# Attention and feed-forward in two layers: four heads of one key tile in one score phase

## The chip, the cores and the metric

The kernel runs on one core of one Trainium2 chip. The metric is the device time of one execution in microseconds (us). TensorE is PE in the profile (its weight loads PEld), VectorE is DVE, ScalarE is ACT, GpSimd is POOL and SyncE, which issues the transfers, is SP.

## The reference

Two layers, each an attention block and a feed-forward block with residuals, over 2048 tokens of width 512 in bf16. Attention has 32 heads of 16 channels and no mask.

```python
def _A_ref(x, wqkv, wo):
    qkv = (x @ wqkv).reshape(B, S, 3, H, Dh)          # H = 32, Dh = 16
    ...
    scores = einsum("bhqd,bhkd->bhqk", q, k) * Dh ** -0.5
    p = softmax(scores, axis=-1)
    o = einsum("bhqk,bhkd->bhqd", p, v)
    return merge_heads(o) @ wo
def _B_ref(x, w1, w2):
    return silu(x @ w1) @ w2
x = A_x
x = x + _A_ref(_layernorm(x), A_wqkv, A_wo)
x = x + _B_ref(_layernorm(x), B_w1, B_w2)
... # the same once more with the same weights
```

## The kernel before

**Blocks.** Attention is cut into blocks: one head, one key tile of 128 keys, one chunk of 512 queries. The scores of a block are one matmul (`score`, L754) with 32 rows of contraction (two heads share 32 rows, and a mask in `QT` picks one of them), which uses one of four row lanes of PE. A block is named by layer L, query chunk qc, pass pi, group of eight heads g, parity par, key tile kt and lane j. A run is all blocks of one (L, qc, pi, g, par): the four heads of lanes 0 to 3 over the key tiles of the pass. There are 4096 blocks: 2 layers x 4 chunks x 8 (g, par) x 16 key tiles x 4 lanes. A pass is all 16 key tiles, except where the keys are not made yet: the first chunk of layer 0 has passes of 4, 4 and 8 tiles, that of layer 1 of 12 and 4.

**Two ways to the exponential.** An A block's scores go to a PSUM tile `s_ps` of two banks (two blocks, two buffers), and ScalarE makes the exponentials with one ACTIVATE of 1024 columns (L1020) into `p_sb`. A D block's scores go to `d_ps` (one bank, two buffers); VectorE makes one fixed-point operation of it (L889, called the fix below), `d_y`, whose bits are read as a half float, and GpSimd adds two offset copies of a pair of these (`d_z0`, `d_z1`, L909). The sum of the three terms, each with its own scaled V (`VA`, and `VB` from `scale_v`), stands for the exponential. So an A block has one PV matmul, and a D block three. PV matmuls (L836) use four column lanes and add up into one bank `o_ps`; a column of ones in V gives the softmax sum. When a run ends, DVE copies `o_ps` (L992, `oT`, or `oA` and `oB` for passes), and PE turns it back (`att`, L467).

**Steps.** `plan` writes 1552 steps by hand: in each, two A blocks of a run, and in 992 of them also a D block, four steps or so ahead of where its run stands, whose lane is free in that step. Every second step or so is followed by PV for the two steps before (`emit_pv`), with terms of D blocks added where they are ready. `emit_pv` also puts in matmuls with zero weights (fills) where PE has had less than `FULL_CLOCK` groups of work since the last PV.

**Background.** All else is made of generators in one queue, `Background`: layer norm (`ln_stats`, `ln_apply`, `ln_transpose`), the projections for K, Q and V (`mm4`: four matmuls in two parts, then a DVE copy), the output projection, the feed-forward block with its 98 tanh on ScalarE (L526; 14 more stand in the tail). Each generator says before each part how much PE or DVE time it takes, and whether it holds the one PSUM bank `m` that all of them share. `Model` keeps an estimate of when each engine will be free, and the loop over steps puts a part into the order only where the model says that it fits before the next exp. What a step needs and what hasn't been made is forced by `Background.ensure`, whatever it costs.

**Order.** The engines work strictly in the order in which the loop emits (a manual schedule). In a step: the sum's copy, DVE parts, scores of the A blocks, score and fix of the D block, PV, PE parts, exp. SP takes its transfers in order as well: Q is brought into place with eight small transfers for each group of heads, `wo` is loaded again for each chunk into the buffer that `hT` and the pass sums (`oB`) use too. The last chunk's output projection and feed-forward form a `tail` after the steps.

Of the kernel before, what the change touches and what calls it, by code (L numbers as in the profile page):

```python
# [26 lines left out]
class Background:  # L27
# [3 lines left out]
    def __init__(self):  # L31
        self.queue = deque()
        self.urgent = deque()
        self.active = None
        self.done = {None}

# [36 lines left out]
    def ensure(self, label):  # L73
        while label not in self.done:
            self.advance(self.prime(self.active or self.queue[0]))

class Model:

    EXP = 0.947
    TANH = 0.66
    SWITCH = 0.09

    def __init__(self, slack, margin):
        self.slack, self.margin = slack, margin
        self.ends = [0.0, 0.0]
        self.pe = self.dve = self.ready = self.free = 0.0
        self.mode = None  # L90
# [6 lines left out]
    def begin(self, d):  # L97
        self.start = max(self.pe, self.ends[0] + 0.06)
        self.d = d

    def dve_fits(self, held, pe, dve):

        if dve == 0:
            if held:
                self.ends[1] = max(self.ends[1], self.ready) + self.TANH
                self.ready = self.ends[1] + 0.05
            return True
        end = max(self.dve, self.start, self.ready if held else 0.0) + dve
        if max(end, self.start + 0.4) + 0.69 * self.d > self.start + self.slack:
            return False  # L110
        self.dve = end
        if held:
            self.free = end
        return True

    def scores(self, d):
        self.pe = self.start
        self.to("S")
        self.pe += 0.25
        self.scored = self.pe + 0.06  # L120
        if d:
            self.dve = max(self.dve, self.pe + 0.1) + 0.69
# [4 lines left out]
    def pv(self, groups):  # L127
        self.to("V")
        self.pe += 0.224 * groups
        self.summed = self.pe + 0.1  # L130

    def pe_fits(self, pe):

        end = max(self.pe, self.free + 0.06) + pe + self.SWITCH * (self.mode != "B")
        act = max(self.ends[1], self.scored) + self.EXP
        if max(end + self.SWITCH, self.ends[1] + 0.06) + 0.31 + self.margin > act:
            return False
        self.pe, self.mode = end, "B"
        self.ready = end + 0.07
        return True  # L140

    def exp(self):
        self.ends = [self.ends[1], max(self.ends[1], self.scored) + self.EXP]

@with_exitstack
def kernel(
# [26 lines left out]
    VW = 17 * H + 16  # L173
    SHIFT = 2.0
# [10 lines left out]
    D_KTS = ((0, 5, 10, 15), (3, 4, 9, 14), (2, 7, 8, 12, 13), (1, 6, 11, 12, 14))  # L185

    FULL_CLOCK = 3


    DVE_SLACK = 2.2  # L190
    PE_MARGIN = 0.1


    STEPS = {16: (24, 23), 12: (20, 20), 8: (12, 12), 4: (7, 7)}
# [11 lines left out]
    ppool = ctx.enter_context(tc.tile_pool(name="ppool", bufs=5))  # L206
# [231 lines left out]
    def d_blocks(c):  # L438

        return [(kt, j) for kt in range(4 * c, 4 * c + 4) for j in range(4) if kt in D_KTS[j]]  # L440

    def scale_v(L, c):

        n = len(d_blocks(c))
        VB[L, c] = vbpool.tile(
            [P, n, 2, 8 * 17 + 16], FP16, name="VB", tag=f"VB{n}", bufs=6 if n == 4 else 1
        )
        nc.gpsimd.memset(VB[L, c][:, :, :, 8 * 17 :], 0.0)
        for i, (kt, j) in enumerate(d_blocks(c)):
            va = VA[L, c][:, kt % 4, 0 : 17 * H].rearrange("p (g j e) -> p g j e", j=4, e=34)  # L450
            for k, (_, w) in enumerate(TERMS):
                nc.gpsimd.tensor_scalar(
                    out=VB[L, c][:, i, k, 0 : 8 * 17].rearrange("p (g e) -> p g e", e=34),
                    in0=va[:, :, j, :],
                    scalar1=w,
                    scalar2=0.0,
                    op0=ALU.mult,
                    op1=ALU.add,
                )
# [217 lines left out]
    def lanes_of(n):  # L677
        return [(n + 3 - j) // 4 for j in range(4)]

    def plan():  # L680

        steps = []
        spans = []
        pv = {}
        for r in runs:
            key, kts = r[0:5], list(r[5])
            t0 = len(steps)  # L690
            t1 = t0 + STEPS[len(kts)][not (0, 1) <= key[0:2] <= (1, 0)]
            left = [len(kts) - m for m in lanes_of(2 * (t1 - t0))]
            d_rows = [[kt for kt in D_KTS[j] if kt in kts][: left[j]] for j in range(4)]
            assert [len(rows) for rows in d_rows] == left
            a_rows = [[kt for kt in kts if kt not in d_rows[j]] for j in range(4)]
            for i in range(0, 2 * (t1 - t0), 2):
                steps.append(([(*key, a_rows[m % 4][m // 4], m % 4) for m in (i, i + 1)], []))
            spans.append((t0, t1, key, d_rows))
            ends = [*range(t0 + 2, t1 - 1, 2), t1]
            for a, b in zip([t0, *ends], ends):  # L700
                pv[b + 1] = list(range(a, b))
        for t0, t1, key, d_rows in spans:
            ts = [t for t in range(max(0, t0 - D_LEAD), t1 - D_LEAD)]
            free = {t: [j for j in range(4) if j not in [b[6] for b in steps[t][0]]] for t in ts}
            n = sum(map(len, d_rows))
            lane = None
            for some in sorted(
                itertools.combinations(ts, n),
                key=lambda some: sum((b - a) ** 2 for a, b in zip((ts[0] - 1, *some), (*some, ts[-1] + 1))),
            ):  # L710
                lane = match(sorted(some, key=lambda t: len(free[t])), free, [len(rows) for rows in d_rows])
                if lane is not None:
                    break
            for t in sorted(lane):
                steps[t][1].append((*key, d_rows[lane[t]].pop(0), lane[t]))
        return steps, pv

    def match(ts, free, left):

        if not ts:  # L720
            return {}
        for j in sorted(free[ts[0]], key=lambda j: -left[j]):
            if left[j]:
                rest = match(ts[1:], free, [m - (k == j) for k, m in enumerate(left)])
                if rest is not None:
                    return {ts[0]: j, **rest}
        return None
# [3 lines left out]
    for ts in pv_steps.values():  # L731
        key = steps[ts[0]][0][0][0:5]
# [29 lines left out]
    def pv_block(blk, k, rhs):  # L762
# [6 lines left out]
        else:  # L769
            h = 2 * g + par  # L770
            i = d_blocks(kt // 4).index((kt, j))
            lhsT = VB[L, kt // 4][:, i, k - 1, 17 * h : 17 * h + 32]
        return (blk[0:5], j, lhsT, rhs)

    def pv_step(t):
        p_sb = p_tiles.pop(t)
        mms = []
        for i, blk in enumerate(steps[t][0]):
            mms.append(pv_block(blk, 0, p_sb[:, i, :]))
        return mms  # L780

    def emit_pv(t, mms, busy):
# [63 lines left out]
        fill = max(0, min(fill, 2))  # L846
# [12 lines left out]
        if ends:  # L859
# [16 lines left out]
            if final[key]:  # L876
                need = ("aT", *((L, qc - 1) if qc else (L - 1, NC - 1))) if (L, qc) != (0, 0) else None
                bg.urgent.append((t + 2, end_group(L, qc, g, par), need))
        return real + fill

    def emit_d(t, blk):

        s_ps = psum["s"].tile([P, 512], FP32, name="d_ps", tag="sd", bufs=2)
# [20 lines left out]
    def other_terms(t, pr):  # L904

        n = len(pr["ds"])
        for k, (off, _) in enumerate(TERMS):
# [9 lines left out]
            for i, d in enumerate(pr["ds"]):  # L917
                d["rhs"].append((t + 4 + k, k + 1, z[:, i, :].bitcast(FP16)))
# [14 lines left out]
    with tc.manual_schedule(  # L933
# [37 lines left out]
        begun = set()  # L971
        busy = 0.0
        m = Model(DVE_SLACK, PE_MARGIN)
        for t, (a_blks, d_blks) in enumerate(steps):
            for L, qc, pi, g, par, kt, j in d_blks + a_blks:
                bg.ensure(("q", L, qc, g))
                if qc == 0:
                    bg.ensure(("k", L, kt // 4, g))
            for L, qc, pi, g, par, kt, j in a_blks:
                if kt % 4 or j > 1 or (L, qc, pi, g, par, kt) in begun:  # L980
                    continue
                begun.add((L, qc, pi, g, par, kt))
                if par == 0 and (kt, g, pi) == (0, 0, 0):
                    attn[L, qc] = apool.tile([P, 4, D], BF16, name="attn", tag="attn")
                    if (L, qc) != (0, 0):
                        next_q(*((L, qc - 1) if qc else (L - 1, NC - 1)), NG - 1)
                first = PASSES.get((L, qc), [range(NKT)])[-1][0]
                if par == 0 and kt == first and g > 0 and final[L, qc, pi, g, par]:
                    next_q(L, qc, g - 1)
            m.begin(len(d_blks))  # L990
            while after:
                after.pop()()  # L992
                m.sums()

            while True:
                item = bg.head(t)
                if item is None or item[2][1] or not m.dve_fits(*item[2]):
                    break
                last = item[2][2] == 0
                bg.advance(item)  # L1000
                if last:
                    break
            s_ps = psum["s"].tile([P, 2, 512], FP32, name="s_ps", tag="s", bufs=2)
# [61 lines left out]
```

The softmax here doesn't subtract the row's maximum and nothing guards it: scores larger than these inputs give would overflow.

## Time and profile before

| | |
|---|---|
| median of three runs | 1609.77 us (1609.59 to 1619.6) |
| span of the profiled execution | 1605.9 us |
| ACT busy | 1514.0 us, 94% |
| PE busy | 1436.8 us, 89% |
| POOL busy | 1098.4 us, 68% |
| DVE busy | 1036.7 us, 65% |
| mean granted clock of PE | 0.986 |
| ACT idle just before exps | 47.4 us |

The profile gives no time of its own for the profiled execution beside its span, which runs from the first to the last instruction; the runs' times are measured around the whole execution, 3.9 us more at the median. An engine's busy time counts overlapping instructions once; neighbours overlap by some 0.1 us on ACT and more on PE, so an instruction's duration is longer than its distance to the next. In a group's row the numbers after the bar are busy time, the mean duration of one in ns, and the engine's idle time just before them with what ended it. A timeline row gives the start, the time covered, the engine, the line, what is written from what, and how many equal neighbours were merged.

### The profile page before, as it was taken

Reading aid. Unit: us, or ns where it says so; the run is one execution under the profiler, and the core shown is the slowest. Engines: PE = TensorE matmul, PEld = TensorE weight load, DVE = VectorE, ACT = ScalarE, POOL = GpSimd, SP = SyncE. Lnnn points to the kernel's source line nnn. Section 1 sums busy time; section 2 is a strip of 40 time slices with the busy share of each in tenths; the row PEclk is TensorE's granted clock in tenths of the full one; section 3 lists DMA queues with packets and bytes.
Section 4 is the critical chain, followed back from the end, with each engine's and each line's share of the span. In section 5 each row is a group of like instructions: output and inputs, shape, how many; then the busy total and the mean of one; then the engine's idle time right before and its main releaser. Section 6 shows DMA issues by size and latency. Waiting matters only on the chain.

```text
span 1605.9 us, 33881 instructions
## 1 busy us (share of the span) xinstructions
PE 1436.8 (89%) x12965; PEld 439.9 (27%) x12965; DVE 1036.7 (65%) x1729; ACT 1514.0 (94%) x1671; POOL 1098.4 (68%) x1160
## 2 busy tenths in 40 slices
PE   7889888899988999889998997888988899988988
PEld 3222222222222222222222222322222222222223
DVE  5566657567776668656664453776678667777644
ACT  6999989999999999999999998999999999999982
POOL 3447767677876778668743452788888788888860
PEclk9999999999999999999999998999999999999999
DMA  4000010101100001100011000100011101100011
GB/s 125 14 14 2 8 44 11 28 8 30 28 21 18 11 27 28 28 14 25 11 37 27 11 17 8 30 21 18 12 31 30 28 8 31 31 21 18 11 28 49
DMA packets 83506, 38.62 MB, mean 24 GB/s; under 512 B 63632, under 2 KB 82832, under 8 KB 83344
## 3 DMA queue, kind: packets, MB, share of 16 engines
q1 hardware_dynamic: 83344, 36.46, 8.6%
q8 instruction: 101, 1.65, 0.4%
q14 instruction: 61, 0.50, 0.1%
HBM read 28.57 MB, written 4.19 MB: 20 GB/s over the span
## 4 chain that ended last, share of the span: by engine, by line
ACT 43%; PE 33%; issue 11%; DVE 10%; DMA 1%; SPq 1%; POOL 1%; ACTq 0%; DVEq 0%
ACT p_sb L1020 40%; PE s_ps L754 10%; PE o_ps L836 10%; PE f_ps L586 4%; DVE d_y L889 3%; ACT t_sb L526 2%; PE h_ps L373 2%; DVE hT L529 1%; PE v_ps L373 1%; DVE xn L310 1%; DVE st L301 1%; PE y_ps L373 1%; PE k_ps L373 1%; PE q_ps L373 1%; SPq L414 1%
## 5 line engine op out<-in xcount | busy, mean ns | idle before, releaser
L1020 ACT ACTIVATE p_sb<-s_ps 128x1024 bf16<-128x1024 f32 x1552 | 1464.9, 1047 | 47.4 <-PE s_ps L754 26.7
L889 DVE TENSOR_SCALAR d_y<-d_ps 128x512 uint16<-128x512 f32 x992 | 674.4, 687 | 376.7 <-PE d_ps L754 338.1
L754 PE MATMUL s_ps<-QT,KT 32*128 32x512 bf16 x3104 | 602.8, 387 | 68.8 <-ACT p_sb L1020 62.6
L754 PE MATMUL d_ps<-QT,KT 32*128 32x512 bf16 x992 | 382.6, 386 | 0.5 <-DVE QT L405 0.5
L754 PEld LDWEIGHTS <-KT 32*128 32x128 bf16 x4096 | 160.7, 91 | 653.5 <-issue 640.8
L836 PE MATMUL o_ps<-p_sb,VA 128*32 128x512 bf16 x3104 | 316.0, 395 | 6.9 <-DVE oT L992 2.6
L836 PE MATMUL o_ps<-d_y,VA 128*32 128x512 f16 x992 | 176.0, 382 | 0.0
L836 PEld LDWEIGHTS <-VA 128*32 128x32 bf16 x4096 | 101.1, 94 | 190.5 <-issue 180.8
L586 PE MATMUL f_ps<-w_sb,hT 128*128 128x512 bf16 x392 | 112.8, 383 | 4.8 <-DVE hT L529 4.8
L836 PE MATMUL o_ps<-w_qkv,zero 128*32 128x512 bf16 x570 | 113.1, 383 | 0.0
L529 DVE SCALAR_TENSOR_TENSOR hT<-t_sb,h_ps 128x512 bf16<-128x512 f32 x98 | 67.3, 687 | 37.6 <-ACT t_sb L526 35.4
L836 PEld LDWEIGHTS <-VB 128*32 128x32 f16 x1984 | 75.4, 98 | 29.6 <-issue 6.0
L526 ACT ACTIVATE t_sb<-h_ps 128x512 f32<-128x512 f32 x98 | 60.3, 615 | 0.0
L992 DVE CAST oT<-o_ps 128x512 bf16<-128x512 f32 x63 | 43.1, 684 | 11.8 <-PE o_ps L836 11.7
L301 DVE BATCH_NORM_STATS2 st<-x 128x6 f32<-128x512 bf16 x64 | 43.4, 678 | 1.9 <-DMA x<-in_A_x_dram 1.9
L373 PE MATMUL y_ps<-wo,aT 128*128 128x512 bf16 x128 | 37.4, 394 | 4.3 <-DMA wo<-in_A_wo_dram 3.9
L373 PE MATMUL v_ps<-w_qkv,xnT 128*128 128x512 bf16 x128 | 37.4, 390 | 3.0 <-DVE VA L431 3.0
L373 PE MATMUL q_ps<-xnT,w_qkv 128*128 128x512 bf16 x128 | 38.1, 398 | 1.4 <-DVE KT L389 1.4
L586 PEld LDWEIGHTS <-hT 128*128 128x128 bf16 x392 | 25.6, 97 | 50.0 <-issue 40.2
L373 PE MATMUL k_ps<-xnT,w_qkv 128*128 128x512 bf16 x128 | 36.1, 382 | 2.9 <-DVE xnT L336 0.9
L467 PE MATMUL att<-ident,oT 128*128 128x128 bf16 x256 | 29.8, 223 | 8.6 <-DVE hT L529 8.3
L332 PE MATMUL t_ps<-ident,xn 128*128 128x128 bf16 x256 | 23.4, 226 | 15.3 <-DVE xn L310 14.9
(2269 smaller groups left out, 2149.0 us busy)
## 6 DMA issues: line engine op xcount, KB each, us to landing
wo<-in_A_wo_dram SPq DMA_DIRECT2D x8, 512.0 KB, 3.9
x<-in_A_x_dram SPq DMA_DIRECT2D x7, 512.0 KB, 4.4
QT<-q SPq DMA_DIRECT2D x224, 16.0 KB, 1.8
out_dram<-x SPq DMA_DIRECT2D x16, 128.0 KB, 1.7
w_sb<-in_B_w_dram SPq DMA_DIRECT2D x1, 1792.0 KB, 13.7
w_qkv<-in_A_wqkv_dram SPq DMA_DIRECT2D x3, 512.0 KB, 7.2
x<-in_A_x_dram SPq DMA_DIRECT2D x2, 256.0 KB, 3.1
x_0_113<-x SPq DMA_DIRECT2D x4, 128.0 KB, 1.8
```

What stands on the lines that cost most here:

```text
L301: nc.vector.bn_stats(st[:], x_sb[c][:, i, :])
L332: nc.tensor.transpose(t_ps[:, ct, u, :], xns[u][:, ct * P : (ct + 1) * P], ident[:, :])
L373: nc.tensor.matmul(ps, lhsT=lhs(ct), rhs=rhs(ct), start=(ct == 0), stop=(ct == CT - 1))
L467: nc.tensor.matmul(att[:, tq, :, :].rearrange("p j s -> p (j s)"), lhsT=o[:, tq * P : (tq + 1) * P], rhs=ident[:, :], start=(i == 0), stop ...
L526: nc.scalar.activation(t_sb, h_ps, ACT.Tanh, scale=0.5)
L529: nc.vector.scalar_tensor_tensor(out=hT[:, ft, :], in0=t_sb, scalar=1.0, in1=h_ps, op0=ALU.add, op1=ALU.mult)
L586: nc.tensor.matmul(y_ps, lhsT=hT[:, ft, tq * P : (tq + 1) * P], rhs=w2_sb[:, ft, :], start=(ft == 0), stop=(ft == FT - 1),)
L754: nc.tensor.matmul(out, lhsT=KT[L, kt // 4][r, g, (kt % 4) * P : (kt % 4 + 1) * P], rhs=QT[g][r, par, :], start=True, stop=True,)
L836: nc.tensor.matmul(o_tiles[key][32 * j : 32 * j + 32, :], lhsT=lhsT, rhs=rhs, start=(n[j] == 0), stop=stop,)
L889: nc.vector.tensor_scalar(out=pr["y"][:, len(pr["ds"]), :], in0=s_ps[:], scalar1=float(1024 * SCALE * math.log2(math.e)), scalar2=float(10 ...
L992: after.pop()()
L1020: nc.scalar.activation(p_tiles[t][:].rearrange("p a b -> p (a b)"), s_ps[:].rearrange("p a b -> p (a b)"), ACT.Exp, bias=-SHIFT * math.log ...
```

## The change

- A step becomes a batch: the four blocks (lanes 0 to 3) of one key tile of a run. There are 1024 batches. The block of lane kt % 4 is always a D block; the three others are A blocks. So 25% of the blocks are D blocks, where it was 24.2%; the first four D blocks are A blocks too, with two 1024-column exps ahead of the loop (`p_pre`).
- PSUM: `s_ps` keeps two buffers of two banks and holds two A blocks; the third A block has a bank of its own, `s1`, with one buffer. `d_ps` has one buffer instead of two. `o` and `m` keep one bank each.
- In each score phase: two matmuls to `s_ps`, one to `s1`, and one to `d_ps`, for the D block four batches ahead. ScalarE then does an exp of 512 columns on `s1` and one of 1024 on `s_ps`, into a `p_sb` tile of three banks' width, four buffers instead of five.
- PV comes every second batch, for the two batches before last. `FULL_CLOCK` goes from 3 to 5 groups and the bound on fills from 2 to 3.
- `Model` has other constants and keeps account of the new banks. Background parts, those of DVE too, are put in after the exps of a batch, and several of one batch may follow each other; parts forced by `ensure` are now charged to the model.
- `VB` is laid out without gaps between terms.

The order of the new kernel's instructions has these counts: 1024 exps of 512 and 1026 of 1024 columns, 1020 D blocks, 1252 fill matmuls (570 before), and the same background work and transfers.

```diff
+    EXP1 = 0.49
+    EXP2 = 0.918
+    TANH = 0.63
...
+    def scores(self, n, d):
         self.to("S")
+        self.pe = max(self.pe, self.s1, self.s2[n % 2])
+        self.scored = self.pe + self.GROUP + self.LAND
         if d:
+            self.pe = max(self.pe, self.sd)
+            self.dve = max(self.dve, self.pe + self.GROUP + self.LAND) + self.FIX
+            self.sd = self.dve + self.SEM
+        self.pe += self.GROUP
...
+    def fits(self, cost):
+        held, pe, dve = cost
+        if pe:
+            end = max(self.pe, self.free) + pe + self.SWITCH * (self.mode != "B")
+            return end + self.SWITCH + self.GROUP + self.LAND + self.margin <= self.act
+        if dve:
+            return max(self.dve, self.ready if held else 0.0) + dve <= self.act + self.slack
         return True
...
-    FULL_CLOCK = 3
-    DVE_SLACK = 2.2
-    PE_MARGIN = 0.1
-    STEPS = {16: (24, 23), 12: (20, 20), 8: (12, 12), 4: (7, 7)}
+    FULL_CLOCK = 5
+    DVE_SLACK = 0.0
+    PE_MARGIN = 0.05
...
-    ppool = ctx.enter_context(tc.tile_pool(name="ppool", bufs=5))
+    ppool = ctx.enter_context(tc.tile_pool(name="ppool", bufs=4))
...
     def plan():
+        blocks = [[(*r[0:5], kt, j) for j in range(4)] for r in runs for kt in r[5]]
+        d_of = [b[b[0][5] % 4] for b in blocks]
+        steps = [(d_of[0:D_LEAD], [])]
         pv = {}
+        for i, b in enumerate(blocks):
+            a = [b[(b[0][5] + k) % 4] for k in (1, 2, 3)]
+            steps.append((a, d_of[i + D_LEAD : i + D_LEAD + 1]))
+            pv.setdefault(i // 2 * 2 + 4, []).extend(
+                [(i + 1, k) for k in range(3)] + [(0, i)] * (i < D_LEAD)
+            )
         return steps, pv
...
-        fill = max(0, min(fill, 2))
+        fill = max(0, min(fill, 3))
...
-        s_ps = psum["s"].tile([P, 512], FP32, name="d_ps", tag="sd", bufs=2)
+        s_ps = psum["s"].tile([P, 512], FP32, name="d_ps", tag="sd", bufs=1)
...
+            s2 = score_pair()
+            s1 = psum["s"].tile([P, 512], FP32, name="s1_ps", tag="s1", bufs=1)
+            for i in range(2):
+                score(a_blks[1 + i], s2[:, i, :])
+            score(a_blks[0], s1[:])
+            for blk in d_blks:
+                emit_d(t, blk)
+            m.scores(t, len(d_blks))
+            while after:
+                after.pop()()
+                m.sums()
+            if t in pv_steps:
+                m.pv(emit_pv(t, pv_step(t), busy))
+                busy = 0.0
+            p_tiles[t] = ppool.tile([P, 3, 512], BF16, name="p_sb", tag="p")
+            exp(p_tiles[t][:, 0, :], s1[:])
+            exp(flat(p_tiles[t][:, 1:3, :]), flat(s2[:]))
+            m.exps(t)
+            while True:
+                item = bg.head(t)
+                if item is None or not m.fits(item[2]):
+                    break
+                m.charge(item[2])
+                busy += item[2][1] / 0.216
+                bg.advance(item)
```

## The prediction

> **What bounds the kernel now.** I read the page first (chain, then groups), then the timelines of ACT and of PE, then windows of 3.4 us for the clock.
>
> ```profile
> ACT 43%; PE 33%; issue 11%; DVE 10%; DMA 1%; SPq 1%; POOL 1%; ACTq 0%; DVEq 0%
> ...
> L1020 ACT ACTIVATE p_sb<-s_ps 128x1024 bf16<-128x1024 f32 x1552 | 1464.9, 1047 | 47.4 <-PE s_ps L754 26.7
> L889 DVE TENSOR_SCALAR d_y<-d_ps 128x512 uint16<-128x512 f32 x992 | 674.4, 687 | 376.7 <-PE d_ps L754 338.1
> ```
>
> ACT and PE share the chain. ACT is busy 94% of the span, but busy is not packed:
>
> ```profile
> 1060.78 0.60 ACT L526 ACTIVATE t_sb<-h_ps 128x512 f32<-128x512 f32 x1
> 1061.25 4.71 ACT L1020 ACTIVATE p_sb<-s_ps 128x1024 bf16<-128x1024 f32 x5
> 1065.77 0.68 ACT L526 ACTIVATE t_sb<-h_ps 128x512 f32<-128x512 f32 x1
> ```
>
> Start to start, five exps take 4.52, that is 0.904 each, though one shows 1.02 (neighbours overlap). A 512-wide tanh takes 0.477 to the next start. Both fit 0.050 fixed plus 0.427 per 512 columns. The exps start at 14.08 and the last at 1559.15, so the stream takes 1546.0. Packed it would be 1552 x 0.904 + 98 x 0.477 = 1449.7, so **96.2 us are lost between exps**: 20.1 up to the 209th exp (222.3, the end of the first query chunk), 76.1 after. Who loses them shows on PE:
>
> ```profile
> 498.12 0.39 PE L754 MATMUL s_ps<-QT,KT 32*128 32x512 bf16 x2
> ...
> 498.44 0.40 PE L836 MATMUL o_ps<-p_sb,VA 128*32 128x512 bf16 x4
> ...
> 498.66 0.39 PE L836 MATMUL o_ps<-d_y,VA 128*32 128x512 f16 x4
> ...
> 498.99 0.39 PE L754 MATMUL s_ps<-QT,KT 32*128 32x512 bf16 x2
> ...
> 499.31 0.60 PE L373 MATMUL h_ps<-fT,w_7555 128*128 128x512 bf16 x2
> ...
> 499.84 0.39 PE L754 MATMUL s_ps<-QT,KT 32*128 32x512 bf16 x2
> ```
>
> A score phase costs 0.32 whether it holds two or three blocks (0.216 of array time and 0.10 for the change of phase); PV costs 0.216 a group of four and 0.12; two background matmuls cost 0.54. Set against the order of the instructions, PE work after the first chunk is 92% of packed ACT time, and 146 of 1343 steps hold over 0.25 us more PE work than their exp lasts. So PE overload makes most of the 76.
>
> **The change, part by part.** All 4096 blocks stay.
>
> *ACT.* 1552 exps become 1024 of two banks, 1024 of one bank and 2 ahead of the loop. No 512-wide exp is in this trace; its bounds are half of a 1024-wide exp (0.452) and the tanh of that shape plus the 0.017 by which a quarter of the exps start late (0.921 for 0.904), 0.494. I take the tanh's own 0.477, the nearest row, since the fixed 0.050 is the same in both rows. Packed: 1024 x (0.904 + 0.477) + 1.8 + 46.7 = 1462.7, so **+12.9** (-13 and +30 at the bounds). The Trainium skill, "ScalarE: Activation LUTs", section "What ACT_TABLE_LOAD costs", speaks against this: an ACTIVATE with a bias pointer takes about 280 ns + 0.833 ns a column, and neighbours overlap by 93 ns. That leaves 187 ns fixed an instruction, and the 498 more would cost +81 net of the columns saved. By it the total below would be 1664; the rows show 50 ns fixed, so I keep theirs.
>
> *PE.* 1552 score phases become 1025 (-527 x 0.32 = -169); PV keeps its blocks but fills grow from 570 to 1252 matmuls (+170 groups x 0.216 = +37). The fourth lane in a score phase isn't in the trace; two lanes and three cost the same to 4 ns, so I take nothing. The upper bound, a whole 0.216 a batch, adds 194 after the first chunk and brings PE to 93% of ACT, where it was; the later losses would then stay near 76, the bound that I keep for them below. After the first chunk PE work falls from 92% to 78% of packed ACT time, and the batches over by more than 0.25 from 146 to 31. Why 0.25: s1 has one bank, so scores of batch t+1 wait for the one-bank exp of batch t (0.60 long), 0.05 more for the semaphore, and 0.49 from there to the next exp (28.17 to 28.66 below), together 1.14 of the 1.381 of a batch. Behind the waiting s1 score stand the fourth score, PV and background on PE, and the next exp. New waits of the score's weight load on PE's own matmuls are for those of two batches before, long done, and p_sb's four buffers are free a batch before they are needed; nothing for either.
>
> *d_ps with one bank.* Scores to fix 0.45, fix 0.69, semaphore 0.05: 1.19 of 1.381. One further DVE operation (0.60 start to start) fits in that wait, two do not; 59 later batches have two or more, and each blocks the fourth score, so PV and background behind it on PE, by up to 0.4. PE's 22% cover that mostly; I charge 5. A group's o_ps copy now ends 0.2 after the next PV wants the bank: 88 groups x 0.1 = 8.
>
> *POOL.* 1020 instead of 992 terms at 1.12: 2.25 a pair in 2.76 of two batches, needed four batches (5.5) later. Hidden; if not, PV waits in PE's queue.
>
> *SP.* The same transfers. Where wo is first loaded, its issue stands behind eight QT transfers (4.94 us) and PE waited 3.9 for it, ACT 5.1; the order of the new kernel leaves 5.5 where some 9.3 are needed, so 4 to 5 stay.
>
> *The opening.* Here the change costs. Projections that a batch needs and that have not been run are forced ahead of it, one after another through the single m bank:
>
> ```profile
> 26.47 0.69 DVE L389 CAST KT<-k_ps 128x512 bf16<-128x512 f32 x1 [1.35 <-PE k_ps L373]
> ...
> 27.21 1.02 PE L373 MATMUL q_ps<-xnT,w_qkv 128*128 128x512 bf16 x4 [0.78 <-DVE KT L389]
> ...
> 28.17 0.39 PE L754 MATMUL s_ps<-QT,KT 32*128 32x512 bf16 x2
> ...
> 28.27 0.75 DVE L405 TENSOR_SCALAR QT<-q_ps,mask_131 128x512 bf16<-128x512 f32 x1 [1.11 <-PE q_ps L373]
> ...
> 28.66 2.14 ACT L1020 ACTIVATE p_sb<-s_ps 128x1024 bf16<-128x1024 f32 x2 [1.91 <-PE s_ps L754]
> ```
>
> Matmuls to copy 1.06, copy 0.69, semaphore 0.05: 1.8 a projection, with ACT idle. The old order forces little (2.0 and 1.9 idle here). The new one puts a quarter of the opening's blocks on DVE (an eighth before), so statistics and copies are held back and then forced at six batches. Batch 5: scores and PV 0.87, the pending V copy until 1.75, two V and a K at 1.8 each, Q's matmuls 0.97: 8.1, less 1.381 and 0.25 = 6.5. By the same unit, batch 37: V's first copy waits behind three statistics (to 4.1), three more V to 9.5, with PV beside the last, K 0.97 and its phase change: 10.9, so 9.2. Batch 65 (two V, two transposes with their normalised rows, a K) comes to 10.8 and costs 9.2; 13 (K and Q behind three statistics), 29 (a transpose and K) and 73 (two V) cost 3.4, 2.4 and 2.4. Sum 33; I add 4 for half clock in these gaps and 4 for ordinary batches: **41 instead of 20.1**. Bounds: 28 (DVE runs ahead) to 55 (each unit at half clock).
>
> *The later stream.* wo 5, clock and the second layer's opening 6, overloaded batches 4 (31 x 0.1 and a little), DVE 5, o_ps 8: **28 instead of 76.1**. Bounds: 12 and 76.
>
> *Sum:* 12.9 + (41 - 20.1) + (28 - 76.1) = **-14.3** on the span of 1605.9. The median of the runs, 1609.77, lies 3.9 above that span, and I carry this over: 1595.5. Head (14.1) and tail (46.7) keep their instructions.
>
> **The clock.** PE is granted half clock after a window with little work:
>
> ```profile
> 1370.70:1374.10 3.40, 2.33 (x30) 0.76 (x30) 1.23 (x2) 3.40 (x5) 2.92 (x3) 0.99 0.00 0
> 1374.10:1377.50 3.40, 3.40 (x30) 0.72 (x28) 1.98 (x3) 2.76 (x4) 1.72 (x3) 0.50 0.00 0
> ...
> 500.20:503.60 3.40, 2.70 (x30) 0.77 (x28) 1.98 (x3) 3.40 (x5) 2.09 (x2) 1.00 0.17 39
> ```
>
> The first number after the width is PE's busy time, the last but two the clock: 2.33 of 3.4 was followed by 0.50, 2.70 was not. A new pair of batches without background (eight slots, gaps up to 0.6) comes to about 2.58 in its leanest window, just above. The Trainium skill ("TensorE: Matmul & The Clock Gate", "HAM oscillation") asks only for no idle gap over about 3.4 us; by that the clock would cost nothing and the total be some 5 lower. But the window at 1370.7 has no such gap and was followed by half clock.
>
> **The rivals.**
> *Packed (faster).* The later stream loses only wo, clock and 1 more: 12. Then 12.9 + 20.9 - 64.1 = -30: 1579.5. For it: PE at 78%. Against: one-bank chains at 1.14 and 1.19 of 1.381.
> *The clock (slower).* If lean windows fall below some 2.4, every second one of about 160 runs at half clock. A pair then needs 2 x 0.54 + 2.3 = 3.4 on PE against 2.76 + 0.25: 0.35 to 0.7 a window, 80 x 0.6 = +48 on my sum: 1643. Place: the stretches without background. For it: the margin of 0.2 us. Against: windows of 2.58 (at 855) kept the clock.
> *PE wasn't what lost the time.* The losses sit in the one-bank hand-overs, and the opening costs 55: 12.9 + 35 - 30 = +18: 1628. For it: slack of 0.19 on d_ps with DVE at 75%. Against: the 146 overloaded steps.
>
> **How the numbers follow.** Forecast 0.48 (own range 1583 to 1612), packed 0.20, clock 0.14, hand-overs 0.18. This kernel's measurement tells about 1% from no change. Below 1593.7 lie the packed case and nearly half of the forecast: 0.42. Above 1625.9 the clock and a third of the hand-overs: 0.20. The rest is 0.38. The range 1572 to 1632 cuts about one in ten at each end, by the bounds of opening and later stream.
>
> **What would show it.** Right: score phases down to 1025; one-bank exps 0.477 apart from the next, gaps of 6 to 9 us on ACT near batches 5, 37 and 65, few gaps after the first chunk, first chunk ending near 232. Wrong: one-bank exps well over 0.477 apart (the ACT term), dense half-clock windows after the first chunk (clock), s_ps or o_ps late behind d_ps with DVE as releaser (hand-overs).

## The result and the profile after

The changed kernel took **1677.76 us** (1672.48 to 1682.12) against 1611.33 for the kernel before on the same chip: 1.0389 times as long, interval 1.0347 to 1.043. The forecast was 1595.5, range 1572 to 1632. The profiled execution took 1676.69, its span is 1674.5.

The page's chain and its groups, as they were shown of the kernel before (busy, mean ns, idle before):

```profile
ACT 47%; PE 38%; DVE 11%; issue 2%; DMA 1%; POOL 0%; DVEq 0%; POOLq 0%
...
L935 ACT ACTIVATE p_sb<-s_ps 128x512 bf16<-128x512 f32 (+1 forms) x2048 | 1489.0, 897 | 104.1 <-PE d_ps L718 62.1
L848 DVE TENSOR_SCALAR d_y<-d_ps 128x512 uint16<-128x512 f32 x1020 | 702.9, 689 | 520.6 <-PE d_ps L718 475.7
...
L468 PE MATMUL att<-ident,oT 128*128 128x128 bf16 x256 | 30.5, 228 | 75.7 <-DVE oT L981 75.6
```

The exps wait 104 us instead of 47. The last row was a small one in the kernel before, and none of its wait was for `oT`:

```profile
L467 PE MATMUL att<-ident,oT 128*128 128x128 bf16 x256 | 29.8, 223 | 8.6 <-DVE hT L529 8.3
```

Now PE stands still for 75.6 us before the `att` products, which wait for `oT` on DVE. The rest by the forecast's method, start to start on ACT less the packed distances (0.904 and 0.477, which are also the medians measured here), in us. "Lost" is what ACT loses between one exp or tanh and the next:

| | before | forecast | after | att later | best |
|---|---|---|---|---|---|
| packed | 1449.7 | 1462.7 | 1462.7 | 1462.7 | 1462.7 |
| lost up to batch 128, the first query chunk | 20.1 | 41 | 63.3 | 60.2 | 38.0 |
| lost behind it | 76.1 | 28 | 88.3 | 46.5 | 45.4 |
| span | 1605.9 | | 1674.5 | 1629.4 | 1604.7 |

"Att later" and "best" are e1 and e12 below. The packed row came out as forecast. Both loss rows are wrong, by 22 and by 60.

What the large one is shows on a timeline of the kernel after, at the end of a run of heads:

```profile
607.41 0.39 PE L718 MATMUL s_ps<-QT,KT 32*128 32x512 bf16 x3
...
607.57 0.37 PE L718 MATMUL d_ps<-QT,KT 32*128 32x512 bf16 x1
...
608.05 0.69 DVE L848 TENSOR_SCALAR d_y<-d_ps 128x512 uint16<-128x512 f32 x1
608.65 0.68 DVE L981 CAST oT<-o_ps 128x512 bf16<-128x512 f32 x1
...
609.39 0.40 PE L468 MATMUL att<-ident,oT 128*128 128x128 bf16 x4 [1.46 <-DVE oT L981]
...
609.72 0.39 PE L718 MATMUL s_ps<-QT,KT 32*128 32x512 bf16 x3
...
610.19 0.60 ACT L935 ACTIVATE p_sb<-s_ps 128x512 bf16<-128x512 f32 x1 [0.48 <-PE d_ps L718]
```

PV of this run ended before 607.41. Its copy `oT` stands on DVE behind the fix of the next batch, and that fix waits for its score (here for an xnT copy too). PE has been given `att` right behind these scores. So PE waits 1.46, the scores at 609.72 come late, and ACT runs dry. In the kernel before, the copy stood ahead of the fix and `att` a step later, 2.65 us behind the end of the copy:

```profile
587.68 0.68 DVE L992 CAST oT<-o_ps 128x512 bf16<-128x512 f32 x1
...
588.28 1.28 DVE L889 TENSOR_SCALAR d_y<-d_ps 128x512 uint16<-128x512 f32 x2
...
591.01 0.40 PE L467 MATMUL att<-ident,oT 128*128 128x128 bf16 x4
```

The change also moved the line `bg.urgent.append((t + 2, ...` to `t + 1`.

To share out the losses, each gap on ACT is put down to the longest wait on PE (other than for ACT) that ended in the gap, in the exp ahead of it or in the 2.5 us before that exp; where there is none over 0.15 us, the gap is called PE work: PE was busy and came late. This is a rough rule, since a short wait can get a long gap. By it 59.1 of the 151.5 us are `att` waiting for `oT`, 51.4 of them behind the first chunk (61 gaps).

### The profile page after: what moved, and what is told of

Read it like the earlier page. It is cut to its first block, busy times and chain, and to the rows that moved or that the text cites. A ratio compares the mean times of both kernels' runs of the same rounds, so it can differ in the third digit from the quotient of the medians.

```text
span 1674.5 us, 34575 instructions
## 1 busy us (share of the span) xinstructions
PE 1444.0 (86%) x13703; PEld 467.0 (28%) x13703; DVE 1065.1 (64%) x1757; ACT 1524.3 (91%) x2169; POOL 1121.1 (67%) x1180
## 4 chain that ended last, share of the span: by engine, by line
ACT 47%; PE 38%; DVE 11%; issue 2%; DMA 1%; POOL 0%; DVEq 0%; POOLq 0%
ACT p_sb L935 44%; PE o_ps L795 11%; PE s_ps L718 10%; DVE d_y L848 5%; PE f_ps L587 5%; ACT t_sb L527 3%; DVE oT L981 2%; PE d_ps L718 2%; PE v_ps L374 2%; PE att L468 2%; PE q_ps L374 1%; PE k_ps L374 1%; PE h_ps L374 1%; PE y_ps L374 1%; DVE st L302 1%
## 5 line engine op out<-in xcount | busy, mean ns | idle before, releaser
L935 ACT ACTIVATE p_sb<-s_ps 128x512 bf16<-128x512 f32 (+1 forms) x2048 | 1489.0, 897 | 104.1 <-PE d_ps L718 62.1
L848 DVE TENSOR_SCALAR d_y<-d_ps 128x512 uint16<-128x512 f32 x1020 | 702.9, 689 | 520.6 <-PE d_ps L718 475.7
L718 PE MATMUL s_ps<-QT,KT 32*128 32x512 bf16 x3076 | 545.8, 391 | 91.4 <-ACT p_sb L935 74.6
L718 PE MATMUL d_ps<-QT,KT 32*128 32x512 bf16 x1020 | 397.1, 389 | 5.3 <-DVE d_y L848 3.1
L718 PEld LDWEIGHTS <-KT 32*128 32x128 bf16 x4096 | 152.9, 91 | 592.4 <-issue 523.6
L795 PEld LDWEIGHTS <-VA 128*32 128x32 bf16 x4096 | 88.0, 96 | 154.4 <-issue 138.4
L587 PE MATMUL f_ps<-w_sb,hT 128*128 128x512 bf16 x392 | 103.9, 382 | 1.0 <-DVE attn L478 1.0
L468 PE MATMUL att<-ident,oT 128*128 128x128 bf16 x256 | 30.5, 228 | 75.7 <-DVE oT L981 75.6
L527 ACT ACTIVATE t_sb<-h_ps 128x512 f32<-128x512 f32 x98 | 76.3, 778 | 0.7 <-PE h_ps L374 0.7
L795 PEld LDWEIGHTS <-zero 128*32 128x32 bf16 x1252 | 34.5, 100 | 36.7 <-issue 4.7
L468 PEld LDWEIGHTS <-oT 128*128 128x128 bf16 x256 | 17.3, 99 | 94.2 <-DVE oT L981 90.1
```

The lines of the kernel that those rows point to most:

```text
L468: nc.tensor.matmul(att[:, tq, :, :].rearrange("p j s -> p (j s)"), lhsT=o[:, tq * P : (tq + 1) * P], rhs=ident[:, :], start=(i == 0), stop ...
L527: nc.scalar.activation(t_sb, h_ps, ACT.Tanh, scale=0.5)
L587: nc.tensor.matmul(y_ps, lhsT=hT[:, ft, tq * P : (tq + 1) * P], rhs=w2_sb[:, ft, :], start=(ft == 0), stop=(ft == FT - 1),)
L718: nc.tensor.matmul(out, lhsT=KT[L, kt // 4][r, g, (kt % 4) * P : (kt % 4 + 1) * P], rhs=QT[g][r, par, :], start=True, stop=True,)
L795: nc.tensor.matmul(o_tiles[key][32 * j : 32 * j + 32, :], lhsT=lhsT, rhs=rhs, start=(n[j] == 0), stop=stop,)
L848: nc.vector.tensor_scalar(out=pr["y"][:, len(pr["ds"]), :], in0=s_ps[:], scalar1=float(1024 * SCALE * math.log2(math.e)), scalar2=float(10 ...
```

## The experiments

Losses below are worked out as in the table; the kernel before ran beside all of them (1611.3 to 1617.3), so ratios are compared across the groups of runs. Gaps and waits are read from the one profiled execution of each kernel.

**e1: the att products a batch later.**

```diff
-                bg.urgent.append((t + 1, end_group(L, qc, g, par), need))
+                bg.urgent.append((t + 2, end_group(L, qc, g, par), need))
```

> The changed kernel with the turning back of a finished run (att) due one batch later, at t + 2 as before the change. Theory A (att stands in PE's queue right behind the scores of batch t + 1, while the copy oT that it reads stands on DVE behind that batch's fix, so PE and then ACT stand still): PE's wait of att for oT falls from 75.6 us to under 5, ACT's losses after the first chunk fall from 88 us by 45 to 55, the time from 1677 to about 1625. Theory B (the losses are those of the one-bank hand-overs s1 and d_ps, and att only fills a hole that is there anyway): the wait of att vanishes but ACT's losses stay within 10 us, and the time stays over 1665.

1631.52 us, ratio 1.0097 (1.0061 to 1.0133): 46 us less by one index. The same place on its timeline:

```profile
592.98 0.68 DVE L981 CAST oT<-o_ps 128x512 bf16<-128x512 f32 x1
...
594.91 0.39 PE L718 MATMUL s_ps<-QT,KT 32*128 32x512 bf16 x3
594.92 0.39 PE L718 MATMUL d_ps<-QT,KT 32*128 32x512 bf16 x1
...
595.24 0.40 PE L468 MATMUL att<-ident,oT 128*128 128x128 bf16 x4
...
595.57 0.39 PE L718 MATMUL s_ps<-QT,KT 32*128 32x512 bf16 x2
```

`att` has no wait in brackets any more, and in the whole trace PE never waits for `oT` before it. Of the 59 us some 13 came back in other gaps (`t_ps`, the transposes that wait for the normalised rows xn, 23.8 instead of 18.9; PE work 31.6 instead of 25).

**e2: the converse, in the kernel before.** The att products a step earlier, and the sum's copy behind the scores and the fix.

```diff
-                bg.urgent.append((t + 2, end_group(L, qc, g, par), need))
+                bg.urgent.append((t + 1, end_group(L, qc, g, par), need))
...
-            while after:
-                after.pop()()
-                m.sums()
...
             m.scores(len(d_blks))
+            while after:
+                after.pop()()
+                m.sums()
```

> The kernel before, with the two places changed as the new kernel has them: att due at t + 1, and the copy of the sum put behind the score phase and the fix. Nothing else. Theory A: some 55 of the 64 runs' ends stall PE by 0.8 to 1.4 us, and PE has less room here, so the time goes from 1611 up by 45 to 75. Theory B: under 10 us.

1685.99, ratio 1.0441 (1.0387 to 1.0495). Its page has the same row as the kernel after:

```profile
L467 PE MATMUL att<-ident,oT 128*128 128x128 bf16 x256 | 30.7, 228 | 51.4 <-DVE oT L1006 50.6
```

So the order costs the old blocks as much as the new ones. With it in both, the packed batches (1677.8) are no slower than the old steps (1686.0).

**e3: slack for DVE parts in the first chunk,** att products as in the change. The change had also set `DVE_SLACK` from 2.2 to 0.

```diff
+            m.slack = 1.4 if (L, qc) == (0, 0) else DVE_SLACK
```

> The changed kernel with more room for background parts on DVE in the first query chunk alone (slack 1.4 instead of 0). Theory A for the opening (statistics and copies are held back by the bound on DVE parts and are then forced at batches 5, 13, 29, 37, 65 and 73): ACT's losses up to batch 128 fall from 63 us to 35 to 45, the time by 18 to 28. Rival (the opening has too much DVE work with a quarter of its blocks there, in whatever order): the losses move to other batches and the time stays within 8 us.

1666.96, ratio 1.0329 (1.0266 to 1.0393). The opening lost 50.7 instead of 63.3: a part of what was expected (35 to 45). The times alone don't show it: the four runs spread from 1658.6 to 1677.9, and the interval overlaps that of the change. The largest gap left, 10.2 us at 140, is a burst with transposes and a K.

**e4: fills back to three groups** on top of e1.

```diff
-    FULL_CLOCK = 5
+    FULL_CLOCK = 3
```

> As e1_att_later, and fills only up to 3 groups between two PVs, as before the change. Clock theory (the lean windows of the new kernel are just above the work that keeps the full clock): without the fills the half-clock windows go from some 20 to over 60 and the time is 15 to 50 us over that of e1_att_later. Rival (the clock drops only in stalls; the fills cost PE time for nothing): within 5 us of e1_att_later.

1687.11, ratio 1.0447 (1.0386 to 1.0509), 56 us over e1 (15 to 50 were expected). Of windows of 3.41 us at half clock, e1 has 21 and this kernel 98. Windows of its trace (width, then busy time of PE, PEld, DVE, ACT, POOL, the clock, DMA share and GB/s):

```profile
957.27:960.69 3.42, 2.38 (x24) 0.60 (x20) 2.85 (x7) 3.42 (x6) 2.91 (x3) 1.00 0.68 191
960.69:964.10 3.41, 3.30 (x24) 1.28 (x23) 2.30 (x4) 2.87 (x5) 3.08 (x5) 0.50 0.02 5
964.10:967.50 3.40, 3.11 (x22) 0.53 (x20) 2.30 (x4) 2.62 (x4) 1.47 (x3) 0.50 0.00 0
```

2.38 busy is followed by 0.50, as 2.33 was in the kernel before, and ACT falls from 3.42 to 2.87. So too little work on PE does cost the clock, and the price is near the rival's 48. It did not decide because the change's fills held it off. The busy time of a window doesn't settle its clock, though. With windows cut where the clock's records change, 66 full-clock windows of the kernel after have 1.7 to 2.4 us of busy time; 52 were followed by full clock and 14 by half. Of those with 2.4 to 2.9, 1 of 65 there was followed by half clock, and 16 of 90 here. None over 2.9 was. What else decides stays open.

**e5: fills behind the parts of forced projections** on top of e1: three matmuls into the next score tile.

```diff
+        def keep_clock():
+            for i in range(3):
+                nc.tensor.matmul(
+                    ahead[0][:, 0, :], lhsT=ident[:], rhs=w_qkv[:, i, 0:D], start=True, stop=True
+                )
...
     def ensure(self, label):
...
             self.charge(item[2])
+            pe = item[2][1]
             self.advance(item)
+            if pe:
+                self.warm()
```

> The kernel with the att products a batch later (1631.5), plus three 512-column matmuls into the next score tile behind each projection part that the score or PV phase forces, so that PE is not idle while VectorE copies the unit out. Theory A (the opening's bursts are long because a forced unit is one bank handed PE to DVE to PE, 1.02 us of matmuls and 0.78 of waiting, and the clock halves on this half-idle PE, to 1.86 and 0.78): the units of the bursts at batches 5 and 37 go back from 2.65 to 1.8 us, three at each and the batch behind them, so the gaps of 10.98 and 13.03 fall to about 7.2 and 10, the losses up to batch 128 from 60.2 to about 53, half-clock windows up to 256 us from 14 to 6 or fewer; time about 1624 us (1620 to 1628). Theory B (the length is in the bank and the copies, or in work that waits behind them, the clock only shows it): units keep their pitch or grow by the fills, losses stay at 58 to 64, time 1629 to 1637.

1624.34, ratio 1.0049 (1.0028 to 1.0071); up to batch 128 53.0 are lost. The time and the losses are theory A's, the gaps are not: 10.2 and 13.3 (7.2 and 10 were expected). A projection has two parts, so fills stood between its halves too, and a unit took 2.45 us at full clock (copies at 23.20, 25.65 and 28.11). The gain came in the batches behind the bursts.

**e10: the fills at the end of a unit only.**

```diff
-            if pe:
+            if pe and not item[2][1]:
```

> The att products a batch later, and the three fill matmuls only behind the second half of a forced projection, where PE waits for the copy; in the earlier run they also stood between the halves and made a unit 2.45 us at full clock. Theory A (half clock is a term of its own in the bursts): units of 1.8 us at full clock, the gaps of 10.98 and 13.03 at batches 5 and 37 become about 7.5 and 10.5, losses up to batch 128 of 47 to 51, time about 1620 us (1617 to 1624). Theory B (what the clock gives back, the fills and the copies that are late take): losses up to batch 128 of 53 to 60, as with the earlier fills, time 1623 to 1631.

1618.04, ratio 1.001 (0.9984 to 1.0037); 47.8 lost up to batch 128: theory A by time and losses, not by the gaps. Units in the burst of batch 37, first of the kernel after, then of e10:

```profile
89.74 1.02 PE L374 MATMUL v_ps<-w_qkv,xnT 128*128 128x512 bf16 x4 [2.84 <-DVE VA L432]
91.55 1.87 PE L374 MATMUL v_ps<-w_qkv,xnT 128*128 128x512 bf16 x4 [0.79 <-DVE VA L432]
94.19 1.87 PE L374 MATMUL v_ps<-w_qkv,xnT 128*128 128x512 bf16 x4 [0.78 <-DVE VA L432]
```

```profile
87.68 1.87 PE L378 MATMUL v_ps<-w_qkv,xnT 128*128 128x512 bf16 x4 [2.19 <-DVE VA L436]
89.34 1.49 PE L963 MATMUL s_ps<-w_qkv,ident 128*128 128x512 bf16 x3
90.62 1.22 PE L378 MATMUL v_ps<-w_qkv,xnT 128*128 128x512 bf16 x4
91.68 0.81 PE L963 MATMUL s_ps<-w_qkv,ident 128*128 128x512 bf16 x3
92.62 1.02 PE L378 MATMUL v_ps<-w_qkv,xnT 128*128 128x512 bf16 x4
93.48 0.81 PE L963 MATMUL s_ps<-w_qkv,ident 128*128 128x512 bf16 x3
```

In the kernel after the units slow from 1.02 of matmuls to 1.87 in the burst itself: PE idles 0.78 of each, and the clock halves. With fills (L963) they recover. The gaps shrank only to 9.2 and 12.1 (7.5 and 10.5 were expected), as each burst's first units are still slow; most of the 12 us came from the batches behind the bursts, where the gaps put down to d_ps (8.5 in e1) are gone. Half-clock windows in the first 256 us fell from 16 to 4.

**e6: e1 and e3 together.**

```diff
+            m.slack = 1.4 if (L, qc) == (0, 0) else DVE_SLACK
...
-                bg.urgent.append((t + 1, end_group(L, qc, g, par), need))
+                bg.urgent.append((t + 2, end_group(L, qc, g, par), need))
```

> The att products a batch later, and VectorE parts may run 1.4 us past ScalarE's planned end while the first chunk of queries is computed. Theory A (the two edits hit different losses): the opening gains the 12.6 us it gained without the later att products (63.3 to 50.7), so losses up to batch 128 are about 48 instead of 60.2 and the time is about 1620 us (1616 to 1624). Theory B (the slack's gain was part of the same att stalls, or VectorE's extra parts now hold up the fixes that the later att products stand behind): losses up to batch 128 of 56 to 62, time 1628 to 1634.

1612.68, ratio 0.9988 (0.9968 to 1.0008): level with the kernel before, 7 us better than theory A had it. 44.5 are lost up to batch 128, the gaps at batches 5 and 37 are 5.7 and 4.9 instead of 11.0 and 13.0: with slack the V copies and statistics are done before the projections are forced.

**e7: e6 with the fills of e5.**

```diff
+            if pe:
+                self.warm()
```

> All three: att products a batch later, slack in the opening, fills behind forced projection parts. Theory A (half clock and late parts are separate terms of the opening): losses up to batch 128 near 42, what the forecast had charged (41), later losses as with the later att products (46), time about 1613 us (1608 to 1618), level with the kernel before. Theory B (with parts drawn ahead there are fewer forced units left to speed up): the better of the two single edits, 1618 to 1624 us.

1617.7, ratio 1.0015 (0.9995 to 1.0035). Neither: the time lies at the edge of theory A's range, but it is 5 us worse than the slack alone (twelve runs of each on one chip), and 53 are lost in the opening, where 42 were expected and the slack alone has 44.5. The profiles overstate this, as the profiled execution was the slowest run of this kernel and the fastest of e6. The likely reason is that fills between the halves lengthen units that no longer run at half clock; e12, without these, bears it out.

**e12: e6 with the fills of e10.**

```diff
+            if pe and not item[2][1]:
+                self.warm()
```

> Slack of 1.4 in the first chunk, att products a batch later, three fills behind the second half of each forced projection. Theory A (half clock costs separately): the eight half-clock windows before 200 us go, the gap of 10.2 at batch 65 becomes 8 to 8.5, losses up to batch 128 fall from 44.5 to 39 to 42, time 1608 to 1610. Theory B (with parts drawn ahead the clock costs nothing that the fills do not take back): 1612 to 1618.

**1608.14**, ratio 0.995 (0.993 to 0.9971): theory A by time, and 0.5% faster than the kernel before. The gap at batch 65 is 9.5, where 8 to 8.5 were expected.

```profile
ACT 63%; PE 27%; DVE 6%; issue 3%; DMA 0%; POOL 0%; DVEq 0%; POOLq 0%
...
L939 ACT ACTIVATE p_sb<-s_ps 128x512 bf16<-128x512 f32 (+1 forms) x2048 | 1493.7, 933 | 44.3 <-PE s_ps L722 24.4
```

The exps wait 44 us instead of 104; the opening lost 38.0 instead of 44.5.

**e11: the slack in the whole kernel,** on top of e1.

```diff
-    DVE_SLACK = 0.0
+    DVE_SLACK = 1.4
```

> The att products a batch later, and VectorE parts may run 1.4 us past ScalarE's planned end in the whole kernel (the change set this constant from 2.2 to 0). Set against the run with the slack in the first chunk alone (1612.7; losses 44.5 up to batch 128, 42.4 behind). Theory A (behind the opening VectorE has room, the slack changes little there): losses behind batch 128 of 38 to 46, time 1609 to 1616. Theory B (the parts drawn ahead stand before the fixes, and the one d_ps bank then holds up PE): d_ps waits on d_y behind the opening grow, losses behind batch 128 above 55, time above 1624.

1776.8, ratio 1.0983 (1.0937 to 1.1028): theory B, and far beyond it; 214 are lost behind batch 128. In the list of waits (total, times, longest):

```profile
PE d_ps L718 <- DVE d_y L848: 81.8, 177, 1.3
```

In e1 this is 2.6, and in e6, which differs from this run only in where the slack holds, 7.9 with 42.3 lost behind batch 128. So the hand-over of the one d_ps bank stalls once DVE parts are drawn ahead of the fixes. It isn't all of the 214: 89 are put down to d_ps and 50 to transposes waiting for xn, and 72 windows run at half clock (7 in e6). The change's 0 is better than 1.4 behind the first chunk, and too strict in it.

**e9: VectorE two batches ahead instead of four,** on top of e1, with two blocks instead of four ahead of the loop.

```diff
-    D_LEAD = 4
+    D_LEAD = 2
...
```

> The kernel with the att products a batch later (1631.5, losses up to batch 128 of 60.2), with the VectorE block of a batch computed two batches ahead instead of four (two blocks instead of four go to ScalarE before the loop). Theory A (the opening loses what its projections cost beyond what a batch has to spare, and the lead only sets the date): the two batches by which every deadline moves back give room for about one part each, the losses up to batch 128 fall by 1 to 4 us, time 1627 to 1631. Theory B (the lead is what forces the bursts: each of the bursts at 5, 13, 29, 37 and 65 stands before a block that VectorE is to score four batches early): each shrinks by up to the 2.76 us of two batches, losses up to batch 128 of 46 to 52, time 1618 to 1624. Theory C (the later terms now reach PV too late and PE waits for POOL): waits on d_z of 10 us or more, time above 1640.

1678.28, ratio 1.0382 (1.033 to 1.0434): none of the three: the time is theory C's, but PE never waits for d_z. The opening lost 61.5, behind it 90. The score phase shows why:

```profile
437.90 0.39 PE L718 MATMUL s_ps<-QT,KT 32*128 32x512 bf16 x3
438.13 0.37 PE L718 MATMUL d_ps<-QT,KT 32*128 32x512 bf16 x1
```

Two key tiles ahead the D block's lane, kt % 4, is one that an A block of this batch uses, so its matmul starts 0.23 later; in the kernel after the two start 0.01 apart (609.72 and 609.73). From the last score matmul before it the median distance is 0.22 here and 0.006 there. Four ahead it is the free lane. The run is no clean test of what the lead forces in the opening, which stays open. It does show the bound that the forecast had for a fourth block that is not free: 0.22 a batch on PE. The 47 us over e1 are the most that this can have cost: behind the opening PE work grew from 26 to 49, but PV's waits for the copies of the sums grew too.

**e8: transposes wait for the planner's DVE backlog,** from batch 450, on top of e7. In e1 13.5 us behind the first chunk are `t_ps` waiting for xn on DVE, which the planner doesn't count.

```diff
         if pe:
-            end = max(self.pe, self.free) + pe + self.SWITCH * (self.mode != "B")
+            end = max(self.pe, self.free, self.dve + self.SEM if late and self.gate else 0.0) + pe + ...
```

> As the run before, and from batch 450 on the planner counts VectorE's backlog before it places the t_ps transposes, which it now places as if xn were there. Theory A: of the 13.5 us of t_ps waits behind xn after the opening, the half that lies behind batch 450 goes, about 6 us: 1607 us. Theory B (transposes drawn later become PE work in overloaded batches): the same time as the run before within 3 us.

1964.23, ratio 1.2163 (1.2127 to 1.2198). Neither: the transposes hardly ever fitted, the background came to a stand, and its work was forced in gaps of up to 40 us, so the 13.5 us were not tested.

**e13: transposes not in the batch that made their xn,** on top of e12.

```diff
+        if late and self.fed == self.batch:
+            return False
```

> As the run with slack, later att products and fills at the units' ends (1608.1; 83.4 lost), and the transposes of normalised rows (t_ps) may not be placed in the batch in which VectorE was given the xn that they read. Theory A (these transposes stand in PE's queue before the next scores while VectorE is still behind a fix, as the att products did): the 12.3 us of t_ps waits after the first chunk go to under 4, losses behind batch 128 from 45 to 35 to 39, time 1598 to 1602. Theory B (the waits come back as PE work of batches that are overloaded later, or as parts forced in the opening): losses of 80 to 88 in all, time 1605 to 1612. Theory C (the parts stall as they did when the transposes waited for the planner's VectorE backlog): above 1640.

1608.93, ratio 0.9955 (0.9937 to 0.9974): theory B. No t_ps gap is left behind the first chunk, but 83.5 are lost as before (83.4): the parts come later and stand as PE work (27 instead of 22) and as a forced V. This wait is a symptom of parts without room, unlike the att wait.

**e14: the planner's ACT costs as measured,** on top of e12.

```diff
-    EXP1 = 0.49
-    EXP2 = 0.918
-    TANH = 0.63
+    EXP1 = 0.477
+    EXP2 = 0.904
+    TANH = 0.477
```

> As the run with slack, later att products and fills at the units' ends, with the planner's costs for ScalarE set to the measured pitches (0.477, 0.904 and 0.477 instead of 0.49, 0.918 and 0.63). Theory A (the 22 us of PE work behind batch 128 are parts that the planner placed because it believed ScalarE busier than it is, 0.027 a batch and 0.153 a tanh): PE-work losses fall to about 15, time 1600 to 1604. Theory B (they are the batches with five PV groups, which no cost of a part changes, and drawing less leaves more to be forced): 1606 to 1614.

1624.42, ratio 1.0042 (1.002 to 1.0064): slower, by neither reason. PE work lost the same (21), but gaps put down to d_ps (15 up to batch 128), t_ps (18), a forced V (6) and `att` behind DVE's copy `q` (6) grew. The 20 us of PE work remain unexplained.

## Why the prediction was wrong

**ACT: right.** One-bank exps start 0.477 before the next (0.476 to 0.494 for nine in ten), and packed time is 1462.7. The fixed time that the Trainium skill ("ScalarE: Activation LUTs", "What ACT_TABLE_LOAD costs") states for an ACTIVATE with a bias pointer gave 1664 in the prediction. The result lies near that figure by chance: these rows keep 50 ns fixed.

**The fourth lane: right.** Scores to PV take 0.32 with four blocks too (at the least 0.324, with three before 0.320); e9 shows what a lane that is not free costs on PE.

**The one-bank hand-overs: right behind the first chunk.** PE waited 3.1 us for the fixes in all, where 5 were charged. For s1 the trace settles it: in the 175 batches behind the first chunk whose scores waited over 0.1 us for ACT to free their bank, ACT lost at most 0.05 each and 0.9 us in all (204 batches and 3.4 us in e1). So the hand-over rival (1628) named the wrong wait. e11 shows that d_ps stalls once DVE parts stand ahead of the fixes.

**The later stream, 28: wrong, the step that failed.** The prediction saw that the o_ps copy now ends late, and charged its neighbour on PE: PV wanting the bank, 8 us. By the sharing-out that cost 0.8. It did not follow the copy to its other reader. `att` had been moved a batch forward and the copy behind the fix, so their distance went from over a step to less than nothing. Measured: 51.4 us behind the first chunk, and 46 us of the time by e1; e2 shows that it needs nothing of the change but this order. What is left without it, 46, is still 18 above the forecast, and here a size was off as well: 13 t_ps waits, for which nothing was charged, and some 26 PE work against the 4 charged for overloaded batches. It isn't 31 batches that lose, but some 200 gaps of 0.13 each on average; why PE comes late in so many stays open. e13 shows that the t_ps waits only stand for missing room.

**The opening, 41: its bursts were right, two terms were too small.** The six gaps were 7.2, 3.7, 2.4, 12.0, 10.3 and 3.3 us where 6.5, 3.4, 2.4, 9.2, 9.2 and 2.4 were charged: 38.8 for 33. Half clock got 4 in all; keeping the clock up saved 12 (e10). "Ordinary batches" got 4; they lost 24.5, of which 7.8 are put down to att and 7.9 to d_ps behind the bursts (the latter roughly, as PE's own waits for the fixes are 3.1). That DVE parts are held back was the forecast's own reason for the bursts; it took the planner's constant as given, though the change had set it from 2.2 to 0, and 16 us of it come back with slack in this one place (e6 against e1).

**The clock: refuted as the main cause, confirmed as a mechanism.** The kernel after has 31 half-clock windows, 18 of them behind 256 us; with att later 5. So most of them came with the stalls and went with them. Of the rivals this one comes nearest in time (1643), but by a term that hardly acted. e4 gives the rival its price. The Trainium skill ("TensorE: Matmul & The Clock Gate", "HAM oscillation") asks for no idle gap of PE over about 3.4 us; behind the first chunk e4 has none, its longest distance from one matmul to the next being 3.0 us, and 70 of its 98 windows lie there.

## What to carry to other kernels

When an instruction is moved later on one engine, list all its readers and look where each stands in its own queue; an engine that meets one of them too early stalls everything behind it in its order (here 75.6 us of PE for one index). Background work that is placed by a planner is part of a change's cost: its constants decide in which batch a consumer meets its producer, so changed constants are to be costed like changed instructions. A forced chain through one bank idles PE for the copy's time, and here the clock halved in its midst; fills belong where PE waits, not between the halves of the work (e10 against e5).

## What the runs showed of the hardware

- Four matmuls of 32 rows that use four row lanes start within 0.01 us of each other where none waits for its bank (609.72 and 609.73); one in a lane in use starts 0.22 later (e9, median).
- Two windows with 2.33 and 2.38 us of PE busy time in 3.4 were followed by half clock, though no two matmuls in them lie over 0.92 us apart; but 52 of 66 windows with 1.7 to 2.4 kept the full clock in the kernel after. Up to two groups of fills fewer in a PV phase took the half-clock windows from 21 to 98 (e4).
- At half clock a projection's four matmuls take 1.87 instead of 1.02 us, but the copy and its semaphore keep 0.78, so a unit grows from 1.8 to 2.65 (kernel after, batch 37).
